# Both sketch tables in one matmul pass, and a first batch that starts with k and keeps q in token order

## The chip, the cores and the metric

The kernel runs on one core of one Trainium2 chip. The metric is the device time of one execution in microseconds (us). The kernel before has three times: 273.32, 271.61 and 270.28 us, median 271.61.

## What is computed

Two blocks follow each other. The first is an attention with a polynomial sketch, for 4 batches, 4 heads, 1088 tokens and 32 columns a head. The second is a mixture of attention experts on its result `x` (4 batches, 1088 tokens, 128 columns, 4 experts of which 2 are chosen for each token).

```python
def phi(x):
    a = np.einsum('rd,bhsd->bhsr', S1, x)
    b = np.einsum('rd,bhsd->bhsr', S2, x)
    return np.einsum('bhsi,bhsj->bhsij', a, b).reshape(*x.shape[:-1], r * r)   # r = 8
q_p, k_p = (phi(q), phi(k))
kv = np.einsum('bhsf,bhsd->bhfd', k_p, v)
z = np.sum(k_p, axis=2)
num = np.einsum('bhsf,bhfd->bhsd', q_p, kv)
den = np.einsum('bhsf,bhf->bhs', q_p, z)[..., None] + 1e-06
x = num / den          # then (batch, token, head * 32)
# experts: logits = x @ w_gate, the two largest, softmax weights of those two;
# for each expert: causal softmax(x wq (x wk)^T / 8) (x wv) wo, weighted and added
```

S1 and S2 come as 64-bit floats; the kernel decodes them on the chip into a high and a low 32-bit part each.

## The kernel before

**How the order is set.** `Plan` (L73) collects jobs. A job has a name, one or more engines that could do it, what it reads, what it makes, and which buffers it holds. Nothing is scheduled at run time: `ORDER` (L21 to L70) is a list of job numbers written out by hand, `a` or `b` choosing the engine, and `run` (L85) issues the jobs in that order. So each engine works through its own instructions strictly in this order, and waits where an input or a buffer is late. A job whose letter chooses the engine `-` is left out. The 40 `dummy` jobs (L245) are such: two matmuls of zeros each, which may be put in or left out. Before, eight of them are in the order, at the start. PSUM has four double tiles (`pair0` to `pair3`), which all matmul results share.

**The batches.** For each batch `prepare` (L413) does the first block and chooses the experts; `batch` (L1219) does the second block in three groups of tokens (384, 384, 320). The expert block is, in this order for a group: `queries` (L952: matmuls with `Mq`, then two predicated copies that pick each token's two experts, L972), `scores` (L986: matmul L997, mask and minimum on VectorE L1009, exponential on ACT L1025, weighing on POOL L1040, turning on VectorE L1045), `values` (L1055: matmuls L1073 against `x` rows in `xra`, `xrb`, `xrc`, fetched back from DRAM), and `outputs` (L1135: matmuls L1144, L1170, L1194, then stores). Preparation of batch b + 1 is mixed into the expert block of batch b. Only the first batch's preparation stands alone, at the head of the program.

**The sketches.** `sketches` (L530) makes the features of k (all batches) and of q. A transposed input lies in SBUF with head and column on the partitions. `sketch` (L502) multiplies 32x32 blocks: for each of 2 tables (high part `SK[:, 0]`, low part `SK[:, 1]`), 4 heads and 4 groups of columns one matmul (L516), the second table added to the first in PSUM. So there are 32 matmuls a sketch, each of which is two records in the trace (32-bit numbers). Then `turn_sketch` (L520, VectorE, two halves) turns the result back, and `features` (L525) multiplies the two sketches of each token into 64 features a head. `sums` (L550, L556) multiplies k's features with v, extended by a column of ones. For batches 1 to 3, `attend_turned` (L679) folds q's denominators into a changed first table `skx`, so that q's sketch needs `skx` in one pass and the low table in another.

**The first batch** (`early`) has a way of its own. k and q are loaded with each row of 34 neighbouring tokens on a partition (L420, 2 pieces each on SP and ACT, q first). Its sketches cut the columns into 8 and 1 parts (64 matmuls each). `attend_rows` (L583) then turns q's features with TensorE (L590, 18 transposes in 5 pieces), multiplies with the sums (`numer`, L613, 18 matmuls with 128 columns of weights), divides on VectorE (L620 to L622), turns `x` (L628) and copies it to `xT` with a change of order (`keep_x`, L630). Tokens then are in order again only when all three parts are done: everything that reads `xT` waits for all of it. `x` is stored to DRAM in 6 pieces (L640, L645), and fetched again as rows (L649). After that `choose_experts` (L797) computes logits (L806), compares them and makes masks; the first group's masks are widened by TensorE (L905), the others go through DRAM (L891, L896).

[...]

Of the kernel before, what the change touches and what calls it, by code (L numbers as in the profile page):

```python
# [21 lines left out]
1 7a 43b 13b 12a 76 0 3 38a 2 87 15a 48 45 77 88 19b 54 74 75 52 4 50 51 27a 78 86 85 53 66 58 34a 79 46 49 59 80 81  # L22
96 98 102b 82 83a 20a 84a 89 101a 22b 97 99b 36a 100a 90 25b 91 65 64 67a 93a 394 92a 109 110a 392 393 107 111 391
108a 112a 14b 56 115 116a 95a 113 114a 103 57 47 94a 395 401 104 105a 402 55 405 406 106a 121 125 404 686 407 122 60
409a 126 117 118 411a 123 124b 400 127 128a 119 403 408a 61 62b 120a 397 6b 68 399 146 147 150 151 152 154 69 153 148
149 70 179 180 184a 684 155 63 183a 182 130 398 129 132 156 158 133 167 157a 396 181 159a 687 168 170 185 186 412 410a
162 413 187 163 164 201 188 189 190a 215 414b 415 202 685 694 131 216 169 208 174 209 416 417 418b 165 166a 203 204a
205 206 191 420a 695 194 11b 195 192 217 421 210 171 136 172 135 173 211a 689 690 218a 219 220 212 213 419a 207 71 691
422 424 423 430 221 222 223 425 426 428a 245 73 214 28b 246 427a 247 248 249a 431 175 250a 251 72 196 318 197a 252 224
225a 226 193 319 322a 432 227 160 161a 429 320 268 267 269 18b 434a 433a 198 321 323a 260 324 291 134 292 137 261 138  # L30
228 293 199 693 692 200 698 699 700 5b 253 276 254 262 176 435 270 702a 704a 701a 255 275 263a 294 277 256a 278 264
279b 688 177 295a 325 703b 257 178a 229 230 231 232b 235a 705 342 265 280 271a 233a 296 272 281 237 236 234a 697 343
344 436 438a 437a 706 24b 39b 297 298 283 273 707a 274 23b 984 284 696 456 266 285 258 259 458 457 708 459 239 286 983
460 709 713a 710 711a 335 714 287a 288 145 289 282 334 462 712a 715 290 336 716 238 351 139 345 346a 347 981 350 359
358 299 300 301 717 718 719 723 337 352 720a 140 141 338a 339 302 340 439 724 360 461 353 354a 725 40b 303 727a 355
304 306a 308a 341 305b 307b 310 472 473 476a 327 463 464 477a 443 309 726a 356 357 441 442 311 312 361 362 475 478 474
479 363 364a 365 326 440 978 977 979 328 314 142 721a 366 501 502 465 16b 8b 494 495 42b 26b 329 330a 348 313 496 497b
367 515 315 516 331 332 349 508 509 510 538 316a 511a 539 541 333 512 467 480 481 517 468 469 487 488 489 722 490b
543a 470 471a 482 542a 544 540 483b 484 44b 368 369 370 485 371 372 373 143 144 486 498 499 980 987 545 728 513 514
374 375 376 378b 380b 377a 381 503 504b 491 446 382 492 451 518a 384 729 730a 519 453 577 379a 383 576 988 505 982 991  # L40
578 500 731a 749 993 612 992 611 750 520 997a 985 450 317 493 521 506 444 507 466 546 553 994a 751 754 996a 995a 568
569 547 554 579 580a 548 616a 570 752 584 615a 617 581 582 385 386 571 585 586 445 555 556a 557 560 561 562 447 549a
550 614 613 522 523 524 618 583 558 559 760 753 527b 33b 240 755 761 572b 573 551 242 574 587 588a 528a 526b 531 563
564a 552 575 565 566 636 525a 529 530 532 589 590 635 637 454 638 619 449 620 628 627 989 990 629 630 631b 643 591 241
243a 621 622 644 645 651 652 623a 646 653 767 762 632 756 757 448 639b 640 654 641 766 655 768 765 656 390 567 769b
624 625 244 642 592 593 986 594 732 657b 658 388 595 596 770b 763 771 772 633 647b 659 648 649 733 597 601a 999 734
598a 599a 735 998 626 600a 1000a 634 603 808 1001 604 602 1002 1003 1004a 605 534 650 1005a 809 1006a 810 787 788 789
790b 811a 1007 1008 1010 535 812 764a 1009 32b 791 389 780 781 736 533 536a 792 660 793 801 802 832 773 774 775 776a
1016 1017 813 814 758 777 833 794 795 782 834 452 783a 784 831 835b 661 662 663 664 665 1018 537 37b 836b 455 666 803
667 668 1020a 785 1011 796 797a 798 799 786 1019b 837 669 673a 778 1021 838 854 387 862 800 671a 1012 1013a 1014b 1015  # L50
672b 670b 675 674 861 863 864 839 840 737 853 1022 855 804a 1023a 738 677 856 676 857a 1024b 846 906 865a 905 866 867
805 806 841 779 759 904 878 847 848 877 908b 909a 910 807 907 678 1042 879 880 911 842b 31b 868 881a 882 883 742 679
849b 739 740 815 816 41b 817 819a 1044 1043 1047 681 843 844 821a 820a 824 1045 850 1046 845 606 1048 1049 818a 822
947 741 884 823 825 858 608 607 609b 869 610 945 859 870 871 872 944 946 913 937 851 948 1130 852 912 914 928 949 950a
915 916a 936 1051 860 873a 874 1053 929 1054 930 931 1129 748 875 938 828 826 1132 827 1134a 1133a 939 876 932b 933
# [1228 lines left out]
```

## Time and profile before

| | |
|---|---|
| times of three runs | 273.32, 271.61, 270.28 us (median 271.61) |
| span of the profiled execution | 268.2 us (its own time is not given; the median is 3.4 us above the span) |
| TensorE | busy 258.7 us, 96% |
| VectorE | busy 207.9 us, 78% |
| POOL | busy 153.1 us, 57% |
| ACT | busy 105.2 us, 39% |
| chain that ended last | TensorE 86% of the span |
| largest groups of TensorE on that chain | values L1073 28%, scores L997 23%, queries L959 9% |
| DMA | 27.38 MB, 80588 packets, 49760 of them under 512 B |

A row of a timeline gives the start in us, the length in us, the engine, the line of the kernel, the operation, the tile that it writes and those that it reads, its shape, and how many instructions were merged. The chain's rows have start, length and place. "PEld" are weight loads. SPq and ACTq rows are DMA issues, not transfers; the table of issues gives the time to landing. A row of groups gives the total busy time and the mean of one in ns, and after the second bar the idle time of the engine before them and who ended it.

### The profile page before, as it was taken

How to read it: one execution, taken by the hardware profiler on the slowest of the kernel's cores; microseconds unless marked ns; L12 is line 12 of the kernel's file. 1: busy time of each engine (PE TensorE's matmuls, PEld its weight loads, DVE VectorE, ACT ScalarE, POOL GpSimd, SP SyncE). 2: the span in 40 equal slices, each digit the busy share in tenths (PEclk: the TensorE clock that was granted, in tenths of full speed). 3: DMA queues.
4: the chain of work that ended last, by engine and by line, in shares of the span. 5: the costliest groups of instructions: out<-in, count | busy, mean ns of one | idle time of the engine just before them, and what ended most of it. 6: DMA issues, size and time to landing. Idle time of an engine off the chain costs nothing.

```text
span 268.2 us, 9721 instructions
## 1 busy us (share of the span) xinstructions
PE 258.7 (96%) x4085; PEld 194.0 (72%) x4085; DVE 207.9 (78%) x529; ACT 105.2 (39%) x284; POOL 153.1 (57%) x243
## 2 busy tenths in 40 slices
PE   5899999999999999999999999999999999999994
PEld 1487576575697795685697795595789865699984
DVE  4788889999969868899986887697896298886252
ACT  2151546266325506443623405333731253554110
POOL 5448159884799537747666744255462842374642
PEclk9999999999999999999999999999999999999999
DMA  6955869806769628801551621706550579403012
GB/s 188 172 142 88 154 150 183 162 2 111 132 136 170 116 62 171 170 5 41 128 91 28 151 61 22 141 13 136 91 122 13 108 140 207 99 4 81 5 32 55
DMA packets 80588, 27.38 MB, mean 102 GB/s; under 512 B 49760, under 2 KB 79520, under 8 KB 80544
## 3 DMA queue, kind: packets, MB, share of 16 engines
q1 hardware_dynamic: 79952, 26.03, 49.7%
q8 instruction: 32, 0.52, 0.9%
q10 hardware_dynamic: 592, 0.72, 0.9%
q14 instruction: 12, 0.10, 0.1%
HBM read 22.22 MB, written 4.52 MB: 100 GB/s over the span
## 4 chain that ended last, share of the span: by engine, by line
PE 86%; DVE 5%; DMA 4%; issue 1%; POOL 1%; ACTq 0%; ACT 0%; DVEq 0%
PE pair L1073 28%; PE pair L997 23%; PE pair L959 9%; PE pair L1194 7%; PE pair L516 4%; PE pair L556 3%; PE pair L1144 2%; DMA in<-in_k_dram 2%; DMA mb<-md 2%; PE pair L613 2%; DVE qs L972 1%; PE pair L756 1%; PE pair L806 1%; POOL agg L1100 1%; PE pair L1170 1%
## 5 line engine op out<-in xcount | busy, mean ns | idle before, releaser
L1040 POOL TENSOR_SCALAR w<-w,rs,sh 128x512 f32<-128x512 f32 (+14 forms) x68 | 56.5, 836 | 38.0 <-DVE rs L1036 36.7
L997 PE MATMUL pair<-xT,qs 128*128 128x384 f32 (+11 forms) x216 | 75.3, 478 | 0.2 <-DVE rs L1036 0.2
L1025 ACT ACTIVATE w<-w,mx 128x320 f32<-128x320 f32 (+14 forms) x68 | 52.4, 771 | 54.4 <-DVE mx L1009 51.1
L1009 DVE CUSTOM_DVE_ANT_0 w<-pair,mask 128x576 f32<-128x576 f32 (+15 forms) x68 | 48.2, 722 | 11.4 <-PE pair L997 10.7
L997 PEld LDWEIGHTS pair<-xT,qs 128*128 128x128 f32 x216 | 38.1, 190 | 24.9 <-issue 10.1
L1045 DVE STREAM_TRANSPOSE AT<-w 128x640 f32<-128x640 f32 (+14 forms) x68 | 50.9, 759 | 6.2 <-POOL w L1040 6.2
L1073 PEld LDWEIGHTS pair<-AT,xra 32*128 32x128 f32 x1136 | 41.6, 185 | 6.1 <-DVE mx L1009 2.3
L1100 POOL TENSOR_TENSOR agg<-agg,mb 128x768 f32<-128x768 f32 (+1 forms) x22 | 34.1, 1560 | 20.4 <-DVE agg L1096 6.4
L1073 PE MATMUL pair<-AT,xra 32*128 32x160 f32 (+5 forms) x1136 | 44.5, 302 | 0.3 <-DVE qs L972 0.2
L192 ACT COPY agg<-pair 128x384 f32<-128x384 f32 (+1 forms) x35 | 14.4, 470 | 58.8 <-PE pair L1073 49.3
L959 PE MATMUL pair<-xT,Mq 128*128 128x384 f32 (+1 forms) x96 | 34.4, 474 | 0.5 <-DVE ch L810 0.5
L525 POOL TENSOR_TENSOR fp<-w 128x576 f32<-128x576 f32 x23 | 27.8, 1224 | 5.4 <-DVE w L520 4.9
L1073 PE MATMUL pair<-AT,xrb 32*128 32x160 f32 (+5 forms) x752 | 26.4, 286 | 0.0
L1073 PEld LDWEIGHTS pair<-AT,xrb 32*128 32x128 f32 x752 | 26.1, 186 | 0.0
L972 DVE COPY_PREDICATED qs<-mb,pair 128x768 f32<-128x768 uint16 (+1 forms) x24 | 23.1, 961 | 3.5 <-DMA mb<-md 2.3
L959 PEld LDWEIGHTS pair<-xT,Mq 128*128 128x128 f32 x96 | 17.3, 190 | 11.0 <-issue 1.8
L1194 PEld LDWEIGHTS pair<-Mo,agg 128*128 128x128 f32 x168 | 20.4, 192 | 2.4 <-issue 1.3
L1194 PE MATMUL pair<-Mo,agg 128*128 128x128 f32 x168 | 21.8, 278 | 0.0
L1096 DVE COPY_PREDICATED agg<-mb,pair 128x384 f32<-128x384 uint16 (+1 forms) x24 | 12.6, 552 | 6.7 <-ACT agg L192 6.6
L1033 POOL TENSOR_SCALAR rs<-zs 128x1 f32<-128x1 f32 x25 | 5.7, 227 | 16.4 <-ACT rs L1031 7.7
L520 DVE STREAM_TRANSPOSE w<-pair 128x576 f32<-128x576 f32 x16 | 11.8, 761 | 4.0 <-PE pair L516 4.0
L516 PE MATMUL pair<-in,SK 32*32 32x288 f32 (+2 forms) x544 | 12.8, 356 | 1.3 <-DVE w L520 0.7
(158 smaller groups left out, 291.4 us busy)
## 6 DMA issues: line engine op xcount, KB each, us to landing
mb<-md SPq DMA_DIRECT2D x7, 576.0 KB, 6.3
xra<-xd SPq DMA_DIRECT2D x16, 192.0 KB, 5.8
xrb<-xd SPq DMA_DIRECT2D x16, 192.0 KB, 5.3
xrc<-xd SPq DMA_DIRECT2D x16, 160.0 KB, 3.5
mb<-md SPq DMA_DIRECT2D x4, 480.0 KB, 5.7
in<-in_k_dram SPq DMA_DIRECT2D x12, 136.0 KB, 3.0
in<-in_q_dram SPq DMA_DIRECT2D x3, 544.0 KB, 5.8
xd<-w SPq DMA_DIRECT2D x12, 136.0 KB, 4.6
```

The source lines that it names most:

```text
L516: nc.tensor.matmul(dst if early else dst.rearrange("p (j t) -> p j t", t=32), SK[rows, 1] if s else first_[rows], part(src[rows], g), star ...
L525: VEC[e].tensor_tensor(out=f, in0=a[:, :, None, R : 2 * R].to_broadcast([128, NJ, R, R]), in1=a[:, :, 0:R, None].to_broadcast([128, NJ, R, ...
L959: nc.tensor.matmul(plan[ps[x]][:, y, 0:w], Mq[:, ((1, 2), (0, 3))[x][y]], plan[xT][:, 64 * t0 : 64 * t1], start=True, stop=True)
L972: nc.vector.copy_predicated(chosen(), rows(c), rows(plan[ps[x]]))
L997: nc.tensor.matmul(plan[p][:, y, 0 : c1 - c0], plan[qs][:, 128 * t : 128 * t + 128], plan[xT][:, c0:c1], start=True, stop=True)
L1009: nc.vector.tensor_tensor_reduce(out=o, in0=src, in1=msk, scale=-1.0, scalar=mx[:, b, i, x - 1 : x] if x else 3e38, op0=ALU.add, op1=ALU.m ...
L1025: nc.scalar.activation(out=a, in_=a, func=ACTF.Exp, bias=mx[:, b, i, last : last + 1], scale=-1.0, accum_out=zs[:, b, i : i + 1])
L1040: nc.gpsimd.tensor_scalar(out=a, in0=a, scalar1=rs[:, b, i : i + 1], scalar2=plan[("sh", b)][:, i : i + 1], op0=ALU.mult, op1=ALU.mult)
L1045: nc.vector.transpose(dst[:, 0 : keys // 32, t], plan[A][:, 0:keys].rearrange("p (j s) -> p j s", s=32))
L1073: nc.tensor.matmul(plan[Vk[g // 2]][:, g % 2, lo : 32 * nt], plan[(f"xr{j // 12}", b)][rows, j % 12], a[rows, j, lo:], start=(j == 0), sto ...
L1100: nc.gpsimd.tensor_tensor(out=a, in0=a, in1=plan[mb][:, 2 * x : 2 * x + 2, 0:w], op=ALU.mult)
L1194: nc.tensor.matmul(plan[p][0:m, 0, 128 * x : 128 * x + 128], plan[agg][:, e, 128 * x : 128 * x + m], Mo[:, e], start=(e == 0), stop=(e == ...
```

## The change

What it does:

- The two tables lie side by side in 48 columns: high part in 0 to 15, low part in 16 to 31, nothing behind. A pass with columns 0 to 31 gives both products at once, in different rows of the result; after turning back, a new job `join` adds the two (on POOL or VectorE). This holds for every sketch of k and for q's of the first batch: 16 matmuls instead of 32 (64 in the first batch). q's sketches of batches 1 to 3 keep two passes (`skx`, then columns 16 to 47).
- In the first batch k is loaded first. q is loaded by heads in token order (four pieces, two on SP, two on ACT), turned in two parts (the first 384 tokens, and the other 704), and sketched, turned back, joined and multiplied to features in these two parts.
- v of the first batch is loaded in rows of up to 9 tokens, with one transfer a quarter; its spread into `vp` is cut by partitions (96 on POOL, 32 on ACT).
- q's features are turned in four pieces of 6, 4, 4 and 4. The numerators' matmuls have 64 columns of weights instead of 128, and there are 36 instead of 18.
- `x` of the first batch is in token order, so each third of it can be used, stored and fetched by itself (`pieces_of` maps each piece to itself).
- `ORDER` is a new list for all jobs. The eight dummies at the start are left out; two dummies stand at the end, behind the last projection.

The core of the diff:

```diff
-    SK = const("SK", [128, 2, 32])
+    SK = const("SK", [128, 48])
...
-        ve.transpose(SK[0:32].rearrange("p n y -> p (n y)"), room(2, 64, F32))
+        for x, part in enumerate((S_hi, S_lo)):
+            ve.transpose(SK[0:32, 16 * x : 16 * x + 32], part)
...
-            for x in range(2):
-                job(f"load q{b}.{x}", ("SP", "ACT")[x], 0.42, lambda e, x=x: by_rows(nc.scalar if e == "ACT" else nc.sync, plan[qin], q, x),
-                    lead, ("qin", b, x), [qin], landing=0.8, rank=-198.5)
+            for x in range(H):
+                job(f"load q{b}.{x}", ("SP", "ACT")[x % 2], 0.7, lambda e, x=x: by_head(nc.scalar if e == "ACT" else nc.sync, plan[qin], q, x),
+                    lead, ("qin", b, 0), [qin], landing=0.95, rank=-198.5)
...
+        qcut = 384 if early else 512
...
-            for o, w, part in cuts:
-                for s in range(2):
-                    for h in range(H):
-                        rows = slice(32 * h, 32 * h + 32)
-                        for g in range(4):
-                            dst = plan[ts[h // 2]][32 * g : 32 * g + 32, h % 2, o : o + w]
-                            nc.tensor.matmul(dst if early else dst.rearrange("p (j t) -> p j t", t=32), SK[rows, 1] if s else first_[rows],
-                                             part(src[rows], g), start=(s == 0), stop=(s == 1))
+            for s, table in enumerate([SK[:, 0:32]] if first_ is None else [first_, SK[:, 16:48]]):
+                for h in range(H):
+                    rows = slice(32 * h, 32 * h + 32)
+                    for g in range(4):
+                        dst = plan[ts[h // 2]][32 * g : 32 * g + 32, h % 2, 0 : 32 * (j1 - j0)]
+                        nc.tensor.matmul(dst if rows_first else dst.rearrange("p (j t) -> p j t", t=32), table[rows], part[rows, g],
+                                         start=(s == 0), stop=(first_ is None or s == 1))
...
+        def join(e, nm, x, j0, j1):
+            a = parts_ab(nm)[:, 2 * x : 2 * x + 2, j0:j1]
+            VEC[e].tensor_tensor(out=a[:, :, :, 0 : 2 * R], in0=a[:, :, :, 0 : 2 * R], in1=a[:, :, :, 2 * R :], op=ALU.add)
...
+                cuts = ((0, 3), (3, NJ)) if early and nm == "q" else ((0, NJ),)
+                sketches(nm, at, lambda: None, (), () if early else lead_fp, cuts)
...
-        fcuts = ((0, 4), (4, 8), (8, 12), (12, 16), (16, 18)) if early else ((0, 8), (8, 16), (16, 18))
+        fcuts = ((0, 6), (6, 10), (10, 14), (14, 18))
...
-                nc.tensor.matmul(plan[t][:, z // 6, c : c + 2 * (D + 1)], f[:, y],
-                                 plan[kvz][:, y % 2].rearrange("p x d -> p (x d)"), start=True, stop=True)
+                for u in range(2):
+                    rows = slice(64 * u, 64 * u + 64)
+                    nc.tensor.matmul(plan[t][rows, z // 6, c : c + 2 * (D + 1)], f[:, y, rows],
+                                     plan[kvz][:, y % 2].rearrange("p x d -> p (x d)"), start=True, stop=True)
...
+        for m, (j0, j1) in enumerate(((0, 3), (3, 6), (6, N8), (N8, NJ))):
+            job(f"store x {b}.{m}", "SP", 0.45, lambda e, c=(j0, j1): store_x(*c), [("xs", b, min(m, 2))], ("xd", b, min(m, 2)), [xs],
+                landing=0.37 * (j1 - j0) if j1 < NJ else 0.2, rank=rank(0.9))
...
-        pieces_of[b] = {n: 0 for n in range(3)}
+        pieces_of[b] = {n: n for n in range(3)}
```

247 lines of the change are left out of this document (122 added, 125 removed).

## The prediction

> **What bounds the kernel now.** I read the page's busy shares and slices first, then the chain of work in order of time, then the engines' timelines of the first 40 us, where nearly all of the change lies.
>
> ```profile
> span 268.2 us, 9721 instructions
> ...
> PE 258.7 (96%) x4085; PEld 194.0 (72%) x4085; DVE 207.9 (78%) x529; ACT 105.2 (39%) x284; POOL 153.1 (57%) x243
> ...
> PE   5899999999999999999999999999999999999994
> ...
> DVE  4788889999969868899986887697896298886252
> ```
>
> TensorE is at 9 from the third slice to the last but one. VectorE stands at 9 in slices 7 to 11 (40 to 74 us), so the first batch has two near-bounds, and later ones one. The chain in time order shows the head:
>
> ```profile
> 2.34 6.25 DMA in<-in_k_dram
> ...
> 8.68 1.37 DVE in L481 x2
> ...
> 14.93 2.04 PE pair L590 x18
> 16.97 2.22 PE pair L556 x72
> 19.19 1.53 PE pair L516 x63
> 20.72 4.18 PE pair L613 x36
> ...
> 49.92 1.53 PE pair L516 x63
> ...
> 103.56 1.69 PE pair L516 x48
> ...
> 261.92 2.47 PE pair L1170 x22
> ```
>
> k arrives at 8.6 us because q goes ahead of it. Then follow k's features, the 18 feature transposes, the sums, the next batch's k sketch and the numerators. The timelines of VectorE and TensorE show where the head ends:
>
> ```profile
> 29.37 0.14 DVE L831 TENSOR_TENSOR ch<-ch 128x12 f32<-128x12 f32 x1
> ...
> 31.15 0.15 DVE L831 TENSOR_TENSOR ch<-ch 128x22 f32<-128x22 f32 x1
> ...
> 32.83 2.20 DVE L972 COPY_PREDICATED qs<-mb,pair 128x768 f32<-128x768 uint16 x2
> ...
> 35.49 1.79 PE L997 MATMUL pair<-xT,qs 128*128 128x64 f32 x8
> ```
>
> The first scores start at 35.49, once the queries are picked. From there to 264.4 TensorE has work behind work. So a microsecond saved counts where it brings the first scores forward, or where it removes TensorE work after them.
>
> **Sketches in one pass, later batches.** A k sketch was 32 matmuls (64 records); it becomes 16. The q sketches of batches 1 to 3 keep two passes, so they change nothing. The q sketch of batch 1 shows a pass by itself, since its two tables have different names:
>
> ```profile
> 38.35 0.77 PE L516 MATMUL pair<-in,skx 32*32 32x288 f32 x32
> 38.86 1.09 PE L516 MATMUL pair<-in,SK 32*32 32x288 f32 x32
> ```
>
> The first pass blocks TensorE for 0.51 us (38.35 to 38.86), the second up to 1.02. Half of 1.53 is 0.77. The k sketches of batches 2 and 3 lie behind the first scores: 2 x 0.77 = 1.5 us off TensorE (bounds 1.0 and 2.0). Each adds two additions of 288 elements, on POOL in these batches. Nearest rows:
>
> ```profile
> L720 POOL TENSOR_TENSOR w<-w 128x144 f32<-128x144 f32 x6 | 2.9, 489 | 1.1 <-DVE rs L1036 1.0
> ...
> L525 POOL TENSOR_TENSOR fp<-w 128x576 f32<-128x576 f32 x23 | 27.8, 1224 | 5.4 <-DVE w L520 4.9
> ...
> L525 DVE TENSOR_TENSOR fp<-w 128x576 f32<-128x576 f32 x9 | 6.6, 756 | 0.1
> ...
> L520 DVE STREAM_TRANSPOSE w<-pair 128x576 f32<-128x576 f32 x16 | 11.8, 761 | 4.0 <-PE pair L516 4.0
> ```
>
> An addition lies between 0.49 (144 elements) and 1.22 (576), so about 0.75 us on POOL and 0.42 on VectorE (half of 0.756, a little more). POOL is 57% busy, and the sums that wait for these features stand well behind in the order: cost 0, at worst 4 x 0.75 = 3.0 where that cover fails.
>
> **Numerators with 64 columns.** 18 matmuls of 128 weights become 36 of 64; 36 records become 72. Rows:
>
> ```profile
> 16.90 2.29 PE L556 MATMUL pair<-vp,fp 128*64 128x33 f32 x72
> ...
> 20.65 4.23 PE L613 MATMUL pair<-kvz,fp 128*128 128x66 f32 x36
> ```
>
> Today's record costs 4.18 / 36 = 0.116 us. The sums, with 64-column weights on alternating halves, cost 2.22 / 72 = 0.031. The new ones have 66 moving columns instead of 33: from 2.2 us to 4.2 (no gain). I take 2.4, near the sums, whose weight shape is the same.
>
> **The dummies go.** The new order drops all of the dummies at the start; two stand behind the last projection, beside the last copies and stores (cost 0: 3.8 us lie there). What they did is visible in the weight loads:
>
> ```profile
> 1.65 0.15 PEld L248 LDWEIGHTS <-idle 128*128 128x128 bf16 x1 [0.28 <-issue]
> ...
> 2.07 0.15 PEld L248 LDWEIGHTS <-idle 128*128 128x128 bf16 x1 [0.28 <-issue]
> ...
> 4.21 0.15 PEld L248 LDWEIGHTS <-idle 128*128 128x128 bf16 x1 [0.28 <-issue]
> ...
> 4.57 0.10 PEld L248 LDWEIGHTS <-idle 128*128 128x128 bf16 x1 [0.22 <-issue]
> ...
> 6.97 0.59 PE L248 MATMUL pair<-idle 128*128 128x512 bf16 x2
> ```
>
> The same matmul comes every 0.42 us up to 4.21, then after 0.36; later two fit in 0.59, pipe included; a load falls from 0.15 to 0.10. So TensorE starts at about half speed and is fast after some 3.1 us without a gap (1.25 to 4.4), and stayed fast over the gap of 1.5 us that follows. In the changed kernel its first work is the k sketch; it then has gaps until the sums. I let it run at half speed until 3.2 us into the sums. The Trainium skill (TensorE: Matmul & The Clock Gate, Part 1: The HAM clock gate) states the same against this change: the array begins at half clock, and about 3.4 us of sustained matmuls release it. By that figure in place of 3.2 the sum would be 0.1 us later; by the trace's spacing the rule holds here.
>
> **The head, step by step.** Loads, from the issue table, and the decode:
>
> ```profile
> in<-in_q_dram SPq DMA_DIRECT2D x1, 256.0 KB, 2.7
> ...
> in<-in_q_dram ACTq DMA_DIRECT2D x1, 288.0 KB, 4.5
> ...
> in<-in_k_dram SPq DMA_DIRECT2D x12, 136.0 KB, 3.0
> ...
> in<-in_q_dram SPq DMA_DIRECT2D x3, 544.0 KB, 5.8
> ...
> 4.20 0.13 DVE L303 TENSOR_SCALAR w<-w 32x32 int32<-32x32 int32 x1
> ...
> 5.46 0.23 DVE L315 STREAM_TRANSPOSE SK<-w 32x64 f32<-32x64 f32 x1
> ```
>
> k now takes q's place: landed by 6.4 (1.94 + 4.5). q comes in four pieces of 136 KB; the last is issued on ACT behind its copy of the tables, near 6.5, so at least 9.5, and I take 10 with the crowd. VectorE: decode from 4.2 at the latest (1.26 us), two transposes (0.45), the memset of the idle tile (0.27), k's halves (0.70, 0.75) and a spread (0.15) end at 7.8. The sketch's first pair is done at 8.3; two transposes back (0.75 each) and an addition: 10.3. q's halves (704 and 384 columns, 0.88 + 0.56, scaled from 512 and 576): 11.75; one feature: 12.5.
> POOL: two features from 10.3 (12.7), v's spread (1152 elements, about 1.2, as a feature), a feature (15.1). Sums: first half at 13.9, at half speed 2 x 1.11 us, to 16.1; the second turns fast at 17.1 and ends at 17.7. Three weight turns (0.66): 18.4. q's features are done at 17.5 on POOL and VectorE (2.4 us of additions and features behind 15.1). 18 transposes (2.04): 20.4. Numerators 0.8, batch 1's k sketch 0.77, numerators 1.6: 23.8, against 24.9 before. VectorE: first division by 22.3, the sketch back (1.5), two divisions (1.9): 25.7. The first third's logits are there by then (transpose 0.35, copy 0.48, matmuls 0.4 behind 23.8), so: turn of logits 0.35, turn of q1's half 0.75, choice 1.35 (from 29.37 as before), its turn 0.33, two turns of logits 0.65, choice 1.2, turn 0.3, picks 2.2: 32.8. The scores follow 0.4 later at 33.2: 2.3 us earlier than 35.49. TensorE itself is through its queries, masks and batch 1's sums by then (2.6 + 0.75 + 0.76 + 2.2 from 25.7: 32.0).
>
> **Waits that are added or moved.** On SP, batch 1's q load stands behind v loads, and the first of these waits for the sums (17.7). Issued near 19, it lands near 24.8 with 5.8 us; VectorE wants it at 26.1, and all of the choice of experts is queued behind it. The cover is 1.3 us; without it each later microsecond is paid in full. The k loads of batch 1 stand behind q's on SP and are needed at 17.5. The x stores go out per third, so the fetches of xra wait for one store; they are wanted some 14 us later, cost 0.
>
> **The sum.** 268.2 - 2.3 - 1.5 = 264.4 us of span. The times shown have no separate time for the profiled execution; the median 271.61 is 3.4 above its span, so 267.8. From each side: 0.5 more on the body, 1.2 less on the numerators and 0.5 on the tables' landing give 265.6; 0.5 less on the body, 1.8 more for the numerators give 270.1.
>
> **Rivals.** (1) *The clock counts the short bursts* of the three sketches and is full when the sums begin. Then these take 1.1 us each and the transposes wait for q's features at 17.1 to 17.5: numerators at 19.2, so 1.2 us less: 266.6. For it: nothing cooled in a gap of 1.5 us. Against it: the dummies needed an unbroken stretch.
> (2) *VectorE becomes the bound of the first batches.* Its margins are thin now:
>
> ```profile
> 68.93 0.86 DVE L1045 STREAM_TRANSPOSE AT<-w 128x704 f32<-128x704 f32 x1
> ...
> 71.82 4.18 PE L1073 MATMUL pair<-AT,xra 32*128 32x192 f32 x96
> ...
> 131.42 0.78 DVE L1045 STREAM_TRANSPOSE AT<-w 128x576 f32<-128x576 f32 x1
> ...
> 132.31 4.18 PE L1073 MATMUL pair<-AT,xra 32*128 32x192 f32 x96
> ```
>
> The last turned scores end 2.0 us and 0.1 us ahead of the sums that need them. Behind the picks VectorE gets half of q1's turn (0.70) and one addition (0.42) more, while TensorE asks earlier. Then the body's 1.5 is lost and 1.1 of the head's 2.3: 271.6 - 1.2 = 270.4.
> (3) *Slower: half speed lasts through the head*, since gaps between numerators, divisions and logits never let TensorE have its unbroken 3 us. All that it does from 17 us doubles: 0.7 + 2.0 + 2.4 + 0.8 + 1.0 + 0.65 + 1.1 + 2.6 = 11 us more, of which some 9 are on the path: 276.8. It decides from about 22 us on (3.8 us lost is the whole gain). Against it: from the sums to the transposes the order has no gap.
> (4) *The new order leaves TensorE waiting* for masks or queries at batch 1 or 2, with no other engine full; it has the price of each wait, 2 to 4 us, and ends near 271.
>
> **How the numbers follow.** My forecast has 0.46 (its own range 266.3 to 269.5), rival 1 0.18, rival 2 0.18, rival 3 0.09, rival 4 0.09. One per cent is 2.7 us, about what a measurement of this kernel can tell. Faster: 0.85 of the forecast, all of rival 1, a tenth of 2 and 4: 0.59. Slower: rival 3 and a little of 4: 0.10. Same: 0.31. The range 265.0 to 271.8 leaves out rival 3 and the best tail.
>
> **What would show it.** First scores near 33 us; sums 0 with a spacing near 0.06 us at first and numerators near 0.033; k sketches of 32 records in 0.5 to 0.8; TensorE with gaps under 2 us in all behind 33. It is wrong if the first scores come after 35.5, if sums or transposes run at half speed past 20, or if VectorE is named as releaser of TensorE for over 2 us.

## The result, and the profile after

The changed kernel is slower: the ratio to the kernel before is 1.037, with a 95% interval of 1.029 to 1.045. The profiled execution took 282.9 us, with a span of 280.7; the kernel before had 270.28 to 273.35 us beside it. Two of the four executions, at 288.6 and 289.3 us with a mean granted clock of 0.97, are left out of the ratio. The forecast was 267.8 (265.0 to 271.8).

The page of the changed kernel, its first lines and the chain:

```profile
span 280.7 us, 9287 instructions
...
PE 257.3 (92%) x3852; PEld 191.9 (68%) x3853; DVE 221.8 (79%) x538; ACT 104.0 (37%) x276; POOL 162.2 (58%) x259
...
PE   0599799999998898969999999999999999999995
...
DVE  4894999989998976997969878798996288994432
...
PE 57%; DVE 15%; DMA 13%; issue 7%; POOL 4%; ACT 2%; SPq 0%; POOLq 0%; DVEq 0%; ACTq 0%
```

TensorE was busy for 258.7 us before and is for 257.3 now, yet its share falls from 96% to 92%, and from 86% of the chain to 57%: the time did not go into more work but into waits and half speed. (DMA has 13% on the chain, mostly the load of the masks; but behind the first scores VectorE waits 1.9 us for that load, and waited 2.3 before, so it does not explain the difference.) The time is lost in two places, the head up to the first scores and the body behind them. TensorE's timeline of the head, which answers to the rows from 14.93 to 35.49 before:

```profile
6.68 2.29 PE L509 MATMUL pair<-in,SK 32*32 32x288 f32 x32 [6.68 <-DVE in L474]
11.91 1.63 PE L509 MATMUL pair<-in,SK 32*32 32x192 f32 x64 [2.94 <-DVE in L480]
...
15.58 4.06 PE L564 MATMUL pair<-vp,fp 128*64 128x33 f32 x72
...
20.90 3.94 PE L600 MATMUL pair<-ident,fp 128*128 128x128 f32 x18
24.76 0.93 PE L626 MATMUL pair<-kvz,fp 128*64 128x66 f32 x24
25.62 0.85 PE L509 MATMUL pair<-in,SK 32*32 32x288 f32 x32
...
35.42 0.82 PE L910 MATMUL pair<-cTa,AT 64*128 64x192 bf16 x8 [1.72 <-DVE ch L815]
...
39.46 0.92 PE L1002 MATMUL pair<-xT,qs 128*128 128x192 f32 x3 [0.17 <-DVE qs L977]
```

The sums take 4.06 us for 72 records (2.29 before) and the 18 transposes 3.94 (2.20 before). k's sketch takes 2.29 us where as many records take 0.85 at 25.62, but part of that is a wait for the second half of k, which VectorE has ready at 7.65. So TensorE runs at half speed up to the numerators, which start at 24.76 (20.65 before, 20.4 forecast). The granted clock in the profile's rows reads 1.00 all the while; the half speed is read off the lengths of the records, and the runs with dummies below bear it out. The first scores come at 39.46 (35.49 before, 33.2 forecast). Behind them, busy time in stretches, once for the kernel before and once for the changed one (columns: stretch, its length, then the busy time of TensorE, its weight loads, VectorE, ACT and POOL, the granted clock, DMA):

```profile
35.49:264.40 228.91, 228.21 (x3487) 173.03 (x3484) 181.81 (x448) 93.71 (x260) 135.47 (x197) 1.00 0.49 96
```

```profile
39.46:276.55 237.09, 229.69 (x3420) 171.70 (x3422) 191.62 (x454) 92.44 (x253) 137.08 (x201) 1.00 0.48 93
```

The body, from the first scores to the last projection, is 8.2 us longer: TensorE stands idle for 7.4 us of it, before for 0.7. VectorE is busy for 9.8 us more in it, though its work is nearly the same. Where that comes from shows in VectorE's and POOL's timelines, at the first choice and at the choice of batch 2:

```profile
31.91 1.16 DVE L840 TENSOR_TENSOR ch<-ch 128x12 f32<-128x12 f32 x1
33.00 0.17 DVE L841 TENSOR_TENSOR ch<-ch 128x12 f32<-128x12 f32 x1
33.11 1.14 DVE L848 TENSOR_TENSOR c6a<-ch 128x6 bf16<-128x6 f32 x1
...
120.34 1.21 DVE L837 TENSOR_TENSOR ch<-ch 128x34 f32<-128x34 f32 x1
121.47 1.18 DVE L838 TENSOR_TENSOR ch<-ch 128x17 f32<-128x17 f32 x1
122.57 1.21 DVE L839 TENSOR_TENSOR ch<-ch 128x17 f32<-128x17 f32 x1
```

```profile
31.86 2.35 POOL L523 TENSOR_TENSOR fp<-w 128x576 f32<-128x576 f32 x2
...
120.22 3.51 POOL L523 TENSOR_TENSOR fp<-w 128x576 f32<-128x576 f32 x3
```

Operations on 6 to 34 columns take 1.1 to 1.2 us, seven times their 0.17, and each ends within 0.2 us of the end of one of POOL's features: three operations of VectorE lie in step with three features of POOL (3.51 / 3 = 1.17). The first choice takes 3.66 us (31.10 to 34.76) instead of 1.35. The masks are late, and TensorE waits 1.7 us up to 35.42 and, behind the choice of batch 2, 2.5 us:

```profile
124.90 1.39 PE L1078 MATMUL pair<-AT,xra 32*128 32x192 f32 x20 [2.54 <-DVE mx L1014]
```

In the profile of the kernel before, POOL had only one operation of 0.33 us beside the first choice, so the first choice could not show this there.

### The profile page after: what moved, and what is told of

The parts are those of the page before. It is cut to its first block, busy times and chain, and to the rows that moved or that the text cites. A ratio compares the mean times of both kernels' runs of the same rounds, so it can differ in the third digit from the quotient of the medians.

```text
span 280.7 us, 9287 instructions
## 1 busy us (share of the span) xinstructions
PE 257.3 (92%) x3852; PEld 191.9 (68%) x3853; DVE 221.8 (79%) x538; ACT 104.0 (37%) x276; POOL 162.2 (58%) x259
## 4 chain that ended last, share of the span: by engine, by line
PE 57%; DVE 15%; DMA 13%; issue 7%; POOL 4%; ACT 2%; SPq 0%; POOLq 0%; DVEq 0%; ACTq 0%
PE pair L1078 19%; PE pair L1002 17%; DMA mb<-md 8%; PE pair L964 4%; PE pair L1199 4%; DVE qs L977 3%; POOL agg L1105 3%; PE pair L564 3%; DMA in<-in_q_dram 2%; PE pair L509 2%; PE pair L1149 2%; DMA AT<-in_moe_wv_dram 1%; PE pair L600 1%; DVE AT L1050 1%; DMA md<-cT 1%
## 5 line engine op out<-in xcount | busy, mean ns | idle before, releaser
L1045 POOL TENSOR_SCALAR w<-w,rs,sh 128x192 f32<-128x192 f32 (+15 forms) x68 | 56.1, 832 | 46.6 <-DVE rs L1041 44.9
L1002 PE MATMUL pair<-xT,qs 128*128 128x384 f32 (+10 forms) x216 | 76.0, 481 | 3.0 <-DVE qs L977 1.2
L1030 ACT ACTIVATE w<-w,mx 128x256 f32<-128x256 f32 (+15 forms) x68 | 52.4, 772 | 64.9 <-DVE mx L1014 48.8
L1050 DVE STREAM_TRANSPOSE AT<-w 128x192 f32<-128x192 f32 (+14 forms) x68 | 51.0, 760 | 6.7 <-POOL w L1045 6.5
L1014 DVE CUSTOM_DVE_ANT_0 w<-pair,mask 128x704 f32<-128x704 f32 (+14 forms) x68 | 48.0, 720 | 5.7 <-PE pair L1002 4.4
L523 POOL TENSOR_TENSOR fp<-w 128x576 f32<-128x576 f32 (+2 forms) x25 | 29.5, 1194 | 0.9 <-DVE w L518 0.4
L1078 PE MATMUL pair<-AT,xrb 32*128 32x160 f32 (+5 forms) x752 | 27.3, 286 | 0.0
L509 PE MATMUL pair<-in,SK 32*32 32x288 f32 (+2 forms) x288 | 9.6, 448 | 9.6 <-DVE in L474 6.7
L1038 POOL TENSOR_SCALAR rs<-zs 128x1 f32<-128x1 f32 x30 | 6.8, 227 | 18.3 <-ACT w L1030 15.7
L192 DVE COPY agg<-pair 128x384 f32<-128x384 f32 (+1 forms) x12 | 6.1, 517 | 11.6 <-PE pair L1078 10.6
```

Of the source, the lines that this page charges most:

```text
L192: (nc.scalar.copy if eng == "ACT" else VEC[eng].tensor_copy)(o, i)
L523: VEC[e].tensor_tensor(out=f, in0=a[:, :, None, R : 2 * R].to_broadcast([128, j1 - j0, R, R]), in1=a[:, :, 0:R, None].to_broadcast([128, j ...
L1002: nc.tensor.matmul(plan[p][:, y, 0 : c1 - c0], plan[qs][:, 128 * t : 128 * t + 128], plan[xT][:, c0:c1], start=True, stop=True)
L1014: nc.vector.tensor_tensor_reduce(out=o, in0=src, in1=msk, scale=-1.0, scalar=mx[:, b, i, x - 1 : x] if x else 3e38, op0=ALU.add, op1=ALU.m ...
L1030: nc.scalar.activation(out=a, in_=a, func=ACTF.Exp, bias=mx[:, b, i, last : last + 1], scale=-1.0, accum_out=zs[:, b, i : i + 1])
L1045: nc.gpsimd.tensor_scalar(out=a, in0=a, scalar1=rs[:, b, i : i + 1], scalar2=plan[("sh", b)][:, i : i + 1], op0=ALU.mult, op1=ALU.mult)
```

## The experiments

Theories. **A**: without the dummies TensorE is at half speed until 24.8 us. **B**: a VectorE operation on two SBUF tiles waits while POOL reads SBUF, so POOL's features hold up the choices. Rivals: **C**, the clock is not the cause; **D**, VectorE is simply too full; **E / I**, the additions that come with the one-pass sketch; **H**, the new order of the body has no time in hand. All ratios are to the kernel before on the same chip (about 270.7 us), with 95% intervals.

### Dummies put back into the changed kernel

```diff
-45 74 0 ... 1 86 ... 90 ...
+1 (eight dummies) 45 74 0 ... 86 ... 90 (four dummies) ...
```

> The changed kernel with twelve dummies put back: the memset of their tile first on VectorE, eight dummies before k's sketch, four behind it. Theory A (half speed until 24.8 us cost the head about 4 us): sums of batch 0 near 2.2 us instead of 4.06, the 18 transposes near 2.1 instead of 3.94, numerators at 20.5 to 21.5 instead of 24.76 (VectorE's last feature then sets them), first scores 35 to 36.5 instead of 39.46, and the time 3 to 4.5 us shorter. Rival C (the clock is not the cause: the head is set by VectorE's and POOL's features): the matmuls get faster and wait instead, numerators no earlier than 24, time within 1 us.

1.040 (1.031 to 1.049), no gain, and not what theory A expected. The head:

```profile
11.82 1.12 PE L510 MATMUL pair<-in,SK 32*32 32x192 f32 x64 [1.94 <-DVE in L481]
...
14.23 3.47 PE L565 MATMUL pair<-vp,fp 128*64 128x33 f32 x72
...
18.97 3.68 PE L601 MATMUL pair<-ident,fp 128*128 128x128 f32 x18
...
34.83 3.57 PE L565 MATMUL pair<-vp,fp 128*64 128x33 f32 x72
```

q's sketches run at full speed (1.12 us), but behind gaps of 1.94 and 0.76 us the sums and transposes are slow again, and a second time the sums of batch 1 at 34.83, behind a wait of 1.73 us; the granted clock of these stretches is 0.60 and 0.55. So half speed is not only a matter of the start: the clock closes again in an order with gaps. The numerators came 2.2 us earlier, the first scores 1.1 us earlier (38.33), and the body lost it again.

### The dummies taken out of the kernel before

```diff
-1 7a ... 12a ... 38a ... 15a ...
+1 7b ... 12b ... 38b ... 15b ...
```

> The kernel before without its eight dummies. Theory A: sums and transposes of batch 0 run at half speed as they do in the changed kernel (the 18 transposes 3.5 to 4 us instead of 2.20, sums 3 to 4 instead of 2.29), first scores 38 to 40 instead of 35.49, time 2.5 to 5 us longer. Rival C: first scores within 1 us of 35.5.

1.0033 (1.0004 to 1.0062): a miss. The kernel before has enough work ahead of its sums to open the clock without dummies:

```profile
7.50 3.23 PE L516 MATMUL pair<-in,SK 32*32 32x32 f32 x144
11.41 3.15 PE L516 MATMUL pair<-in,SK 32*32 32x32 f32 x112 [0.69 <-DVE w L520]
...
17.74 2.29 PE L556 MATMUL pair<-vp,fp 128*64 128x33 f32 x72
```

The sketches are slow (6.4 us, where the kernel before takes 4.6), but at 17.74 the sums run at full speed, and the first scores come at 36.14, 0.65 us later. By the ratio, leaving the dummies out costs 0.1 to 1.7 us. In the changed kernel the shorter sketches and the missing dummies come together; that the two together leave TensorE too idle to open its clock fits these runs, but the sketches were not lengthened there by themselves.

### POOL writes instead of reading

```diff
+            if e == "POOL" and not early:
+                for _ in range(2):
+                    nc.gpsimd.memset(f, 0.01)
+                return
             VEC[e].tensor_tensor(out=f, ...)
```

> The changed kernel in which POOL, where it makes the features of batches 1 to 3, writes a constant twice instead of multiplying two tiles (so these features, and the output, are not the reference's): POOL stays about as busy but reads nothing there. Theory B (a small VectorE operation on two SBUF tiles waits for the end of a POOL operation that reads SBUF): the first group's choice takes 1.3 to 1.6 us instead of 3.66, the 1.1 us operations at 120 to 124 us fall to 0.1 to 0.2, TensorE's wait of 2.54 us at 124.9 goes, and the time is 4 to 7 us shorter. Rival D (VectorE is simply too full in the new order, or slower beside any POOL work): choice still over 3 us, time within 1.5 us.

1.017 (1.010 to 1.023), 276.0 us: theory B holds, D falls. POOL is as busy as in the changed kernel (159.8 us against 162.2), the first choice takes 1.35 us (29.85 to 31.20), first scores come at 36.21 instead of 39.46, and the body is 233.84 us instead of 237.09. TensorE's head:

```profile
20.61 2.98 PE L604 MATMUL pair<-ident,fp 128*128 128x128 f32 x18
23.52 0.92 PE L630 MATMUL pair<-kvz,fp 128*64 128x66 f32 x24
...
36.21 2.43 PE L1006 MATMUL pair<-xT,qs 128*128 128x192 f32 x10
```

Not all of the 3.25 us of earlier first scores is the choice's. Up to the numerators this kernel does the same work as the changed one, but in this execution the clock opened within the transposes (2.98 us instead of 3.94), and the numerators start at 23.52 instead of 24.76. From the numerators to the first scores it is 12.69 us instead of 14.70: the choice is worth 2.0 us of the head. In the body the reading is worth 3.25 us. VectorE's busy time there falls from 191.6 to 187.4 us, against 181.8 before, so POOL's features explain less than half of its growth.

### The same work of POOL, put into the kernel before

```diff
         def exponents(e, t0, t1):
+            if early and t0 == 0:
+                for _ in range(4):
+                    nc.gpsimd.tensor_tensor(out=JB, in0=JA, in1=JA, op=ALU.mult)
```

> The kernel before with four products of 128x576 of a scratch tile added on POOL ahead of the first exponents (about 4.7 us, from 27.7 on), so that POOL reads SBUF while VectorE makes the first choice. Theory B: the first group's choice takes 3 to 4.5 us instead of 1.35, single operations last about 1.1 us and end with POOL's, and the first scores come 2 to 3 us later than 35.49. Rival D (VectorE is only too full): the choice stays under 1.6 us, and the first scores move by under 0.5.

The second kernel has `nc.gpsimd.memset(JB, 0.01)` twice in place of each product:

> As the kernel before with scratch work on POOL beside the first choice, but POOL writes a constant eight times (about the same time) and reads nothing. Theory B: choice 1.3 to 1.6 us, first scores within 0.5 us of 35.49. If any POOL work holds VectorE: choice over 2.5 us as in the version that reads.

Reading, POOL's row and two of VectorE's:

```profile
28.08 4.81 POOL L858 TENSOR_TENSOR JB<-JA 128x576 f32<-128x576 f32 x4
```

```profile
30.57 1.13 DVE L837 TENSOR_TENSOR ch<-ch 128x6 f32<-128x6 f32 x1
...
31.88 1.05 DVE L846 TENSOR_TENSOR c6a<-ch 128x6 bf16<-128x6 f32 x1
```

Writing, the same operations under a POOL that is as busy:

```profile
30.77 5.02 POOL L858 MEMSET JB<- 128x576 f32 x8
```

```profile
32.68 0.17 DVE L837 TENSOR_TENSOR ch<-ch 128x6 f32<-128x6 f32 x1
...
33.03 0.18 DVE L846 TENSOR_TENSOR c6a<-ch 128x6 bf16<-128x6 f32 x1
```

The one execution of each took 277.1 us (reads) and 273.7 us (writes). With reads the choice takes 3.8 us, TensorE waits 2.15 us for it, the clock closes and the sums of batch 1 take 4.06 us; the first scores come at 40.99, more than expected. With writes the choice takes 1.2 us. The first scores, expected within 0.5 us of 35.49, come at 38.96, because the numerators were late already (23.73, at a granted clock of 0.50 from 13 to 17 us). From the numerators to the first scores it is 14.8 us before, 15.2 with writes and 20.0 with reads. The Trainium skill (SBUF — State Buffer, Who interferes with whom) states just this: a VectorE instruction with two SBUF inputs contends with a GpSimd instruction that reads SBUF, not with one that only writes it. The four rows agree (1.13 and 1.05 us against 0.17 and 0.18).

### Both repairs together

```diff
+            (POOL's features of batches 1 to 3 as constants, as above)
+1 (eight dummies) 45 ... 90 (nine dummies) ... (two dummies) 61 ...
```

> The changed kernel with both repairs: POOL's features of batches 1 to 3 write a constant (twice, same POOL time, not the reference's output), and nineteen dummies so that TensorE has no long gap ahead of the sums (eight first, nine behind k's sketch, two ahead of the repeated S2). Theory A+B: sums of batch 0 about 2.3 us and transposes about 2.2, numerators at 20 to 21.5, first scores 33 to 34.5 instead of 36.21, time 2 to 3 us under the 276.0 of the version with constants alone, that is 273 to 274. If the clock closes again in the gaps that stay (rival F: this order leaves TensorE too idle ahead of 14 us): sums over 3 us and no gain.

1.0105 (1.005 to 1.016), 274.0 us, as expected. The head is now fast:

```profile
15.40 2.29 PE L569 MATMUL pair<-vp,fp 128*64 128x33 f32 x72
...
19.74 2.08 PE L605 MATMUL pair<-ident,fp 128*128 128x128 f32 x17 [0.61 <-DVE fp L528]
21.74 0.92 PE L631 MATMUL pair<-kvz,fp 128*64 128x66 f32 x24
...
34.44 2.43 PE L1007 MATMUL pair<-xT,qs 128*128 128x192 f32 x10
```

The numerators start at 21.74: 1.8 us earlier than in the version with constants alone, whose clock opened within the transposes, and 3.0 us earlier than in the changed kernel. From there to the first scores it is 12.70 us, as with constants alone. So half speed in the head cost the profiled execution of the changed kernel 3.0 us, and the choice 2.0. This is no chance of one execution: in all five kernels with the nineteen dummies the numerators start between 21.74 and 21.89. The transposes now wait 0.9 us in two pieces for VectorE's features of q, six operations that take 4.09 us beside POOL's additions and features; from the mean of 756 ns for 576 elements before I estimate 2.3 for them undisturbed, which was not tried. The body is still 233.36 us.

### The one-pass sketch alone, in the kernel before

```diff
-SK[rows, 1] if s else first_[rows]
+SKP[rows] if first_ is None else SK[rows, 1] if s else first_[rows]
...
+                nc.gpsimd.tensor_tensor(out=a[:, :, :, 0 : 2 * R], in0=a[:, :, :, 0 : 2 * R], in1=a[:, :, :, 2 * R :], op=ALU.add)
```

> The kernel before with the k sketches of batches 1 to 3 alone in one pass (a table with both parts side by side, additions on POOL), order unchanged. The prediction's term: 3 x 0.77 = 2.3 us less on TensorE, time 1.5 to 2.5 us shorter. Rival E (the additions make features and choices late): no gain, 0 to 3 us longer.

The second kernel does it for batches 2 and 3 only (`b > 1`):

> The kernel before with the k sketches of batches 2 and 3 alone in one pass, batch 1 as it was. The prediction's term of the body: 2 x 0.77 = 1.5 us less, 269.0 for 270.5. If additions on POOL, ahead of the features, make features and choices late here as they did with batch 1 (rival E): no gain, or 1 to 4 us longer with a named wait of TensorE for POOL's features or VectorE's choice.

1.027 (1.020 to 1.033) and 1.026 (1.020 to 1.032), over what even rival E expected: in the second kernel the term of 1.5 us less became 7 us more. POOL's and TensorE's timelines of the second kernel at batch 2:

```profile
51.86 1.56 POOL L525 TENSOR_TENSOR w<-w 128x288 f32<-128x288 f32 x2 [2.44 <-DVE w L522]
...
55.66 3.96 POOL L530 TENSOR_TENSOR fp<-w 128x576 f32<-128x576 f32 x3
```

```profile
59.67 2.14 PE L561 MATMUL pair<-vp,fp 128*64 128x33 f32 x36 [3.38 <-POOL fp L530]
61.74 3.57 PE L1002 MATMUL pair<-xT,qs 128*128 128x480 f32 x4
```

In the kernel before the features begin at 52.28, these sums take 1.24 us and start at 56.58, and the scores behind them take 1.88. Now the two additions (1.56 us) stand in POOL's queue ahead of the small work on the experts' weights. POOL stands idle for 2.44 us until VectorE has turned the sketch back, time in which it did that small work before; the features begin at 55.66 and end at 59.6. TensorE waits 3.38 us, and behind that gap it runs at half speed for 5 us (granted clock 0.50). The wait (3.38), the sums (0.90 longer) and the scores (1.69 longer) make 6.0 us at this one place; a wait of 1.5 us ahead of batch 3's choice is most of the rest. Additions placed behind the small work were not tried.

Then the first half of batch 2's sums (705) next to the second (706):

```diff
-705 342 ... 436 ... 706
+342 ... 436 ... 705 706
```

> As the kernel before with the k sketches of batches 2 and 3 in one pass, and the first half of batch 2's sums moved behind two scores, products and numerators, to just ahead of its second half. Theory E' (the additions delay POOL's features by about 3.4 us, TensorE's wait for them and the half speed behind that gap are the whole loss): the wait of 3.38 us and the half speed at 59 to 65 us go, and the 1.5 us of sketches come out: 268.5 to 270 instead of 277.9. If the loss is spread over VectorE and POOL: still over 273.

1.014 (1.009 to 1.018), about 274.5 us where the theory had 268.5 to 270: half of the loss stays. The waits from 55 to 64 us (waiting line and releaser, us in all, times, longest):

```profile
PE pair L761 <- DVE agg L1101: 2.6, 1, 2.6
DVE rs L1041 <- POOL rs L1038: 2.0, 1, 2.0
```

With the sums later the wait moved: TensorE waits for VectorE's masked copies, these stand behind small reciprocals in VectorE's queue, and the reciprocals wait for a guard that is queued behind the features on POOL. POOL's queue itself is on the path.

And the one-pass sketches without what follows them:

```diff
-                nc.gpsimd.tensor_tensor(out=a[:, :, :, 0 : 2 * R], in0=a[:, :, :, 0 : 2 * R], in1=a[:, :, :, 2 * R :], op=ALU.add)
```

> The kernel before with the k sketches of batches 2 and 3 in one pass and no additions (features use the high part alone), so that only TensorE's part of the change is left. The prediction's term: 1.5 us less, 269.3 for 270.8; with it the additions cost all of the 7 us between 277.9 and that. If the halved sketches by themselves close the clock or only make TensorE wait: within 0.5 us of before.

0.9986 (0.9955 to 1.0017): without the additions there is neither a loss nor a gain clear of noise, so the additions and what queues behind them are the 7 us. The profiled execution was the longest of twelve (273.2 us), but it lost that in the head, which the edit does not touch (first scores at 39.01). From there to the last projection it takes 228.9 us, and the kernel before 229.1: TensorE is busy for 1.3 us less, and idle for 1.1 us more. At both sketches it waits right behind for VectorE, 0.36 us at batch 2 and 0.31 us at batch 3:

```profile
54.50 2.23 PE L999 MATMUL pair<-xT,qs 128*128 128x448 f32 x6 [0.36 <-DVE mx L1011]
...
108.01 1.12 PE L808 MATMUL pair<-xT,wg 128*32 128x288 f32 x16 [0.31 <-DVE AT L1047]
```

### The narrow numerators alone, in the kernel before

```diff
+                for u in range(2):
+                    rows = slice(64 * u, 64 * u + 64)
+                    nc.tensor.matmul(plan[t][rows, ...], f[:, y, rows], ...)
```

> The kernel before with the numerators in matmuls of 64 columns of weights alone. The prediction's term: 4.2 us of numerators become 2.4; the divisions on VectorE come 1 to 1.8 us earlier and so do the first scores: time 0.8 to 1.8 us shorter. Rival G (VectorE's divisions and turns set the head): 0 to 0.5 us shorter.

The second has one dummy ahead of each of 123, 127 and 119 (the turns of x):

> As the kernel before with numerators of 64 columns, and one dummy ahead of each of the three turns of x, where TensorE waits 0.6 us for each division. Theory A' (the time taken off the numerators became gaps, and the gaps closed the clock for the 5 us behind them): turns and logits behind 27 us run at full speed again (logits 1.13 us instead of 1.97), first scores 34.5 to 35.3 instead of 37.02, time 0.5 to 1.2 us under before. Rival G: VectorE sets the head, first scores 35.4 to 36, no gain.

1.0032 (0.9996 to 1.0068), and with three dummies 0.998 (0.995 to 1.001). The numerators do fall to 2.51 us. But then TensorE waits for each division, and behind three short gaps the clock closes:

```profile
21.32 2.51 PE L615 MATMUL pair<-kvz,fp 128*64 128x66 f32 x72
24.44 0.55 PE L630 MATMUL pair<-ident,w 128*128 128x128 f32 x3 [0.61 <-DVE w L624]
25.57 0.55 PE L630 MATMUL pair<-ident,w 128*128 128x128 f32 x3 [0.58 <-DVE w L624]
26.73 0.55 PE L630 MATMUL pair<-ident,w 128*128 128x128 f32 x3 [0.62 <-DVE w L624]
...
29.14 1.97 PE L808 MATMUL pair<-xT,wg 128*32 128x192 f32 x24
```

The logits at 29.14 take 1.97 us, at a granted clock of 0.55; with a dummy in each gap they take 1.13. The first scores then come at 35.32 instead of 37.02, but 0.9 us of that lie ahead of the numerators, which the dummies do not touch. From the numerators' start to the first scores it is 14.84 us before, 15.70 with narrow numerators and 14.94 with the dummies as well. So rival G holds: VectorE's divisions set the head, and of the 1.7 us saved on TensorE nothing remains.

### Order or additions: what is left of the body

The version with both repairs is varied in two ways: the order of the body (the changed kernel's, or that of the kernel before from the second score on, with the first half of batch 2's sums next to the second), and the additions of batches 1 to 3 (in, or left out). The first of these kernels still has POOL multiply the features.

```diff
-(the changed kernel's job numbers behind the second score of batch 0)
+(the same jobs in the sequence of the kernel before, joins behind their backs)
...
         def join(e, nm, x, j0, j1):
+            if not early:
+                return
```

> The changed kernel with the nineteen dummies of the head, its own order up to the second score of batch 0, and from there the order of the kernel before (each addition right behind its turn back; first half of batch 2's sums next to the second half). POOL multiplies features as in the changed kernel. Theory H (the body's loss is the new order: choices beside POOL's features and no time in hand for masks): from first scores to TensorE's end 228 to 231 us instead of 237.1, first scores near 37 (choice still beside features), time 271 to 275. Rival (the loss comes with the additions, whatever the order): 235 or more from first scores to the end, time over 277.

> The changed kernel with constants for POOL's features and nineteen dummies (274.0 us; from first scores to TensorE's last projection 233.4 us), and now the additions of batches 1 to 3 left out (k's low part is not added, the features use the high part alone). Theory I (the additions on POOL and what queues behind them make the rest of the body's loss): 228 to 230 us from first scores to the end, time 268.5 to 270.5. Rival H (the new order has no time in hand for masks and choices, additions or not): 232.5 or more, time 273 to 274.5.

> The changed kernel with constants for POOL's features and nineteen dummies, its own order up to the second score, and the order of the kernel before behind it, additions in. Rival H (order): 228 to 230 us from first scores to the end, time 269 to 270.5. Theory I (additions): TensorE still waits over 2 us near 61 us and runs at half speed behind it; 232.5 or more, time over 272.5.

> As the one with the old order of the body, without the additions of batches 1 to 3. Either theory alone leaves a part; with both causes away the prediction's body is left: 227 to 228.5 us from first scores to the end (228.9 before, less 1.5 for the halved sketches), time 268 to 269.5. If neither is the cause: over 231.

| | additions in | additions out |
|---|---|---|
| new order | 1.0105 (1.005 to 1.016), body 233.4 us | 1.016 (1.012 to 1.021), body 236.8 |
| order before | 1.0085 (1.005 to 1.012), body 233.2 | 0.994 (0.989 to 0.998), body 228.6 |

The first kernel, where POOL reads, has 1.019 (1.015 to 1.023) and a body of 234.9, so H alone was wrong there. It differs from the one at the lower left of the table only in that POOL reads, and shows the price of that once more, 2.0 us of first scores (with the numerators at 21.75 and 21.79) and 1.7 us of body:

```profile
36.45 1.79 PE L1003 MATMUL pair<-xT,qs 128*128 128x64 f32 x8 [0.17 <-DVE qs L978]
```

```profile
34.48 1.79 PE L1007 MATMUL pair<-xT,qs 128*128 128x64 f32 x8
```

Either cause alone keeps 4.6 us or more in the body; with both away, it comes down:

```profile
34.59:263.14 228.55, 227.34 (x3423) 172.01 (x3422) 181.86 (x448) 93.84 (x260) 134.02 (x212) 1.00 0.48 96
```

In the old order the additions cost by POOL's queue (VectorE waits 2.3 us for POOL there, TensorE 2.1 for VectorE). In the new order without them the body grows by 3.4 us, and the time is longer than even rival H expected. 3.1 us of that come at one place: TensorE waits 2.1 us up to 57.36 for a masked copy of VectorE, and its clock closes behind that (granted 0.68 from 57 to 60 us). With the additions in, the same matmuls start at 55.51, although VectorE's rows ahead of them are the same. Why they wait for the later operation here is not shown, so the table does not price the new order cleanly.

## Why the prediction was wrong, step by step

- *"I let it run at half speed until 3.2 us into the sums"* failed. Half speed lasted until 24.8 us, through 10 us of gapless small matmuls, sums, weight turns and transposes. The rule by time (3.1 us of the dummies' row) did not carry over to these instructions, nor does a clock once open stay open. It cost 3.0 us: the numerators start at 24.76, and at 21.74 with the dummies. Rival 3 came nearest, with a chance of 0.09 and a price three times too high (9 us); but it looked for the cause in gaps between the numerators and later work, and half speed ended at the numerators, after just the stretch without a gap that was put down against it.
- *Choice 1.35 us, additions and features "cost 0"* failed, and is the largest error: 2.0 us in the head and 3.25 in the body. I asked whether POOL had time for its work, not what its work does to VectorE beside it. Rival 2 named the engine, but by its sum of work.
- *VectorE and POOL through q's features* failed: the last features that the transposes wait for came at 19.7 us even at full clock (17.5 forecast), and the numerators at 21.74 (20.4 forecast). That is 1.3 us of the head. The same contention is the likely reason (4.09 us for what I estimate at 2.3), but POOL's work of the first batch was not exchanged in any run.
- *"2 x 0.77 = 1.5 us off TensorE"* failed. 32 records do take 0.77 us, and an addition takes 0.78 us on POOL (1.56 / 2), near the 0.75 forecast. But the body was not "work behind work" in the sense that a saving counts: VectorE was 0.4 us behind, and the additions stood ahead of POOL's operations on which VectorE's queue waits. Old order with additions: 4.6 us lost.
- *The new order* was taken to keep the body dense except for rival 4 (0.09). Its body has 5 us of idle TensorE even with constants for POOL and the dummies, so rival 4 had the kind of loss right. Whether that part is the order's own or the additions' is not settled, since leaving the additions out of it brought another wait; which of its ten waits of 0.2 to 0.9 us costs the time stays open too.
- Numerators of 2.4 us were right in size (2.51 alone), but worth nothing to the first scores, as the run with them alone shows. The earlier k was right (sketch at 6.68; 7.8 forecast).
- The time around the span was mis-sized too: 2.2 us (282.9 less 280.7) for the changed kernel, where the sum had 3.4. And the sum of the head has a slip: 20.4 and 0.8, 0.77 and 1.6 are 23.6, not 23.8.

Head 6.3 us late = 3.0 (clock) + 2.0 (first choice) + 1.3 (q's features). Body 9.7 us over the forecast (237.1 against 228.9 - 1.5) = 3.25 (choices) + 0.5 (233.8 to 233.4 with the dummies) + 4.8 (additions and order together, 233.4 to 228.6) + 1.15 (savings given back to VectorE and the rest).

With all these causes away the time is 268.9 us, a ratio of 0.994 (0.989 to 0.998): 1.9 us under the kernel before, where the forecast was 3.8 under it. First scores come at 34.59 (33.2 forecast) and the body is 228.6 us (227.4 forecast). That kernel has the old order in its body and leaves out work (the low part of the tables, POOL's features), so no run shows the forecast's gain. How much of the gain a better order could reach stays open.

## What to carry to other kernels

Before an operation is costed at nothing because its engine has time, look what runs beside it: POOL work that reads SBUF can hold a small VectorE operation on two SBUF tiles until the POOL instruction ends, here for up to 1.2 us, so it must not lie beside a chain of such operations on the path. A TensorE instruction that is removed leaves a gap if the next input is not earlier too, and gaps of half a microsecond to two among short matmuls can cost as much again at half clock; fill them, or save first on the engine that comes next (which was not tried here). In an order written by hand, an insertion is priced by everything queued behind it on its engine.

## What the runs showed of the hardware that was not expected

- TensorE's clock closed in the middle of work: behind gaps of 1.94 and 0.76 us with 1.12 us of sketches between (granted clock 0.60), behind one wait of 1.73 us (0.55), and behind three of 0.6 us with 0.55 us of transposes between (0.55). The Trainium skill (TensorE: Matmul & The Clock Gate, Part 1: The HAM clock gate) lets it close after an idle window of about 3.4 us; these stretches were shorter and partly busy, so the measurement decides: a thinly filled stretch is enough, sometimes.
- It opened late under work that is nearly gapless, though the dummies of the kernel before opened it in 3.1 us. In the changed kernel it took 10 us, from 14.6 to 24.8. In the kernel without dummies it took some 8 us, from 7.50 to about 15.5 with one gap of 0.69 us: four turns at 14.49 still take 1.11 us (0.60 before), and the 18 transposes behind them 2.41 (2.20 before). The Trainium skill (TensorE: Matmul & The Clock Gate, Part 4: PE-mode transpose) says that transposes do not count as busy in the same way. The sums ahead of the transposes were slow as well, and no run tells the two apart.
- It is not the same in each execution. The changed kernel and the one in which POOL writes have the same work up to the numerators, and their 18 transposes took 3.94 and 2.98 us. In nine profiles of the kernel before and its variants with eight dummies, whose TensorE work up to the numerators is the same, these start between 20.3 and 24.0 us. So a difference of a few tenths of a microsecond between two heads, each seen once, shows nothing.
